# Attention into expert FFNs: q scaled on DVE, reciprocals spread by TensorE, one casting load queue, program order

## The chip, the cores and the metric

One core of one Trainium2 chip. The time is the device time in microseconds (us) of one execution. Engines: PE is TensorE (matmul), PEld its weight loads, DVE is VectorE, ACT is ScalarE, POOL is GpSimd, SP is SyncE. "Block j" means the FFN of expert 0 on 512 tokens; a block's start is the first matmul into `h_ps` of that block, FFN1 are its matmuls into `h_ps` and FFN2 those into `y_ps`. The releaser of a wait is what ended it. The granted clock is the share of the full TensorE clock that the profile shows. An attend computes a piece of `xT` for one batch. A slot is a place between two groups of FFN matmuls where other work may be put.

## The reference, cut to what matters

```python
# q, k, v: (8 batches, 8 heads, 576, 64);  E = 8 experts, Dm = 512, F = 1024, N = 4608 tokens
q_p = concat(relu(q) * cos, relu(q) * sin)       # 128 features; k_p alike; cos, sin depend on the position
kv  = einsum('bhsf,bhsd->bhfd', k_p, v);  z = k_p.sum(over positions)
num = einsum('bhsf,bhfd->bhsd', q_p, kv); den = einsum('bhsf,bhf->bhs', q_p, z) + 1e-6
x   = num / den                                   # then (B*S, H*D) = (4608, 512)
P   = exp(x @ w_gate);  P = sinkhorn(P, 8 rounds) # over all 4608 tokens
out = sum over e of P[:, e] * (relu(x @ w1[e]) @ w2[e])
```

The routing needs the gates of all tokens, so the FFNs of experts 1 to 7 can't be weighted before attention is finished. The kernel therefore runs expert 0, unweighted, while attention is still being prepared.

## The kernel before

Batch b+1 and b+2 are prepared while the FFN of block b runs. The parts that matter are these.

```python
# turn: q is transposed and multiplied by cos / sin in one go, by half-width matmuls
for c in range(i * C3, (i + 1) * C3):
    for a in range(2):
        nc.tensor.matmul(out=t_ps[a * D : (a + 1) * D, ...], lhsT=q16[:, c, :], rhs=cs_diag[:, c, a, :], ...)
# ... then relu from PSUM into q_pT, on ACT and DVE by turns

# denominators: 96 rows x 192 reciprocals, copied to 128 partitions by a trip through DRAM
nc.vector.reciprocal(out=den[:], in_=den[:])
for j in range(3):
    nc.scalar.dma_start(out=r_dram[:, j, :], in_=den[32 * j : 32 * j + H, :])
rb = acc_hi[...]                       # borrowed from the tail of the output accumulator
for hh in range(2):
    nc.scalar.dma_start(out=rb[hh * HP : (hh + 1) * HP], in_=r_dram[hh : H : 2]. ... .to_broadcast([HP, HK, S]))

# attend: xT = num * rb
nc.vector.tensor_tensor(out=xT[...], in0=num_ps[...], in1=rbs[b][...], op=ALU.mult)

# loads: q cast to fp16 by the GpSimd queue, k and v as fp32 on the SP queue, 4 buffers each;
# the weights of expert 0 stand in the GpSimd queue between the q loads of batch 0 and batch 1
```

The order of the instructions on each engine is left to a scheduler, which does not keep the order of the program text.

The softmax here doesn't subtract the row's maximum and nothing guards it: scores larger than these inputs give would overflow.

Of the kernel before, what the change touches and what calls it, by code (L numbers as in the profile page):

```python
# [9 lines left out]
FP32 = mybir.dt.float32  # L10
# [12 lines left out]
def kernel(  # L23
# [39 lines left out]
    ps_h = ctx.enter_context(tc.tile_pool(name="ps_h", bufs=3, space=bass.MemoryType.PSUM))  # L63
    ps_y = ctx.enter_context(tc.tile_pool(name="ps_y", bufs=2, space=bass.MemoryType.PSUM))
    ps_s = ctx.enter_context(tc.tile_pool(name="ps_s", bufs=3, space=bass.MemoryType.PSUM))

    xT = xT_pool.tile([P, KT, N], F16, name="xT")

    G_LO = NG - 8
    acc_lo = acc_pool.tile([P, G_LO, Dm], FP32, name="acc_lo")  # L70
    acc_hi = acc_pool.tile([P, NG - G_LO, Dm], FP32, name="acc_hi")

    def acc(g):
        return acc_lo[:, g, :] if g < G_LO else acc_hi[:, g - G_LO, :]
# [3 lines left out]
    def load_weights(pool, e, cuts):  # L78
        w1e = pool.tile([P, KT, F], F16, name="w1e")
        w2e = pool.tile([P, FT, Dm], F16, name="w2e")  # L80
        v1 = moe_w1[e].rearrange("(kt p) f -> p kt f", p=P)
        v2 = moe_w2[e].rearrange("(ft p) d -> p ft d", p=P)
        for i in range(cuts):
            f0, f1 = i * F // cuts, (i + 1) * F // cuts
            nc.gpsimd.dma_start(out=w1e[:, :, f0:f1], in_=v1[:, :, f0:f1])  # L85
        for i in range(cuts):
            f0, f1 = i * FT // cuts, (i + 1) * FT // cuts
            nc.gpsimd.dma_start(out=w2e[:, f0:f1, :], in_=v2[:, f0:f1, :])  # L88
        return w1e, w2e


    def ffn1(hT, w, j, fts=range(FT)):
        for ft in fts:
            h_ps = ps_h.tile([P, TCH], FP32, name="h_ps")
            for kt in range(KT):
                nc.tensor.matmul(  # L96
                    out=h_ps[:],
                    lhsT=w[0][:, kt, ft * P : (ft + 1) * P],
                    rhs=xT[:, kt, j * TCH : (j + 1) * TCH],
                    start=(kt == 0),  # L100
                    stop=(kt == KT - 1),
                )
            nc.scalar.activation(out=hT[:, ft, :], in_=h_ps[:], func=AF.Relu)  # L103

    def ffn2(hT, e, w, j, tss=range(TCH // P)):
        for ts in tss:
            g = j * TCH // P + ts
            y_ps = ps_y.tile([P, Dm], FP32, name="y_ps")
            for ft in range(FT):
                nc.tensor.matmul(  # L110
                    out=y_ps[:],
                    lhsT=hT[:, ft, ts * P : (ts + 1) * P],
                    rhs=w[1][:, ft, :],
                    start=(ft == 0),
                    stop=(ft == FT - 1),
                )
            if e == 0:

                if g % 2 == 0:
                    nc.scalar.copy(out=acc(g), in_=y_ps[:])  # L120
                else:
                    nc.vector.tensor_copy(out=acc(g), in_=y_ps[:])
            else:
                nc.vector.scalar_tensor_tensor(  # L124
# [12 lines left out]
    with ExitStack() as p1:  # L137
        cs_pool = p1.enter_context(tc.tile_pool(name="cs_pool", bufs=1))
        ld = p1.enter_context(tc.tile_pool(name="ld", bufs=4))
        kp_pool = p1.enter_context(tc.tile_pool(name="kp_pool", bufs=3))  # L140
        va_pool = p1.enter_context(tc.tile_pool(name="va_pool", bufs=3))
        qT_pool = p1.enter_context(tc.tile_pool(name="qT_pool", bufs=8))
        kv_pool = p1.enter_context(tc.tile_pool(name="kv_pool", bufs=2))

# [3 lines left out]
        def load(b, hk):  # L148
            t = []
            for name, src, dt, eng in (  # L150
                ("q", q, F16, nc.gpsimd), ("k", k, FP32, nc.sync), ("v", v, FP32, nc.sync),
            ):
                x = ld.tile([P, C, D], dt, name=f"{name}_ld")
                view = src[b].rearrange("(hk hh) (p c) d -> (hh p) hk (c d)", hh=2, c=C)
                eng.dma_start(out=x[:].rearrange("p c d -> p (c d)"), in_=view[:, hk])  # L155
                t.append(x)
            loaded[b, hk] = t

        for hk in range(HK):
            load(0, hk)  # L160


        half_pi = cs_pool.tile([P, 1], FP32, name="half_pi")
        nc.vector.memset(half_pi[:], float(np.pi / 2.0))
# [5 lines left out]
        )  # L170
        wrap = cs_pool.tile([P, C], FP32, name="wrap")
        nc.vector.tensor_scalar(
# [3 lines left out]
        nc.vector.scalar_tensor_tensor(  # L176
# [6 lines left out]
        nc.scalar.activation(out=cs[:, :, 0, :], in_=s_b, func=AF.Sin, bias=half_pi[:], scale=-ang)  # L183
        nc.scalar.activation(out=cs[:, :, 1, :], in_=s_b, func=AF.Sin, scale=ang)
        ident = cs_pool.tile([P, P], F16, name="ident")
        nc.gpsimd.memset(ident[:], 1.0)
        nc.gpsimd.affine_select(
            out=ident[:], in_=ident[:], pattern=[[-1, P]], compare_op=ALU.is_equal,
            fill=0.0, base=0, channel_multiplier=1,
        )  # L190

        cs_diag = cs_pool.tile([P, C, 2, P], F16, name="cs_diag")
        nc.vector.tensor_tensor(  # L193
            out=cs_diag[:].rearrange("p c a s -> p (c a) s"),
            in0=ident[:].unsqueeze(1).to_broadcast([P, 2 * C, P]),
            in1=cs[:, :, :, 0:1].rearrange("p c a o -> p (c a) o").to_broadcast([P, 2 * C, P]),
            op=ALU.mult,
        )
# [3 lines left out]
        nc.vector.memset(zmask[:], 0.0)  # L202
        for h in range(H):
            nc.vector.memset(zmask[:, h, h : 32 : H], 1.0)
        ones_col = const.tile([P, 1], FP32, name="ones_col")
        nc.vector.memset(ones_col[:], 1.0)
        scale_row = const.tile([1, 2, P], FP32, name="scale_row")
        nc.vector.memset(scale_row[:, 0, :], float(N) / float(E))
        nc.vector.memset(scale_row[:, 1, :], float(N) / float(E) / XS)
# [3 lines left out]
        nc.vector.tensor_copy(out=wg[:], in_=wg_ld[:])  # L213

        w0 = load_weights(wA, 0, 4)


        kps, qTs, kvs, rbs = {}, {}, {}, {}

        def prep(b, hk):  # L220
            _, k32, v32 = loaded[b, hk]
            v_aug = va_pool.tile([P, C, D + 2], F16, name="v_aug")
            nc.vector.tensor_copy(out=v_aug[:, :, 0:D], in_=v32[:])  # L223
            nc.vector.memset(v_aug[:, :, D : D + 1], 1.0 / XS)
            k16 = kp_pool.tile([P, C, D], F16, name="k16")
            nc.scalar.activation(out=k16[:], in_=k32[:], func=AF.Relu)
            k_p = kp_pool.tile([P, C, 2, D], F16, name="k_p")
            nc.vector.tensor_tensor(  # L228
                out=k_p[:], in0=k16[:].unsqueeze(2).to_broadcast([P, C, 2, D]),
                in1=cs[:], op=ALU.mult,  # L230
            )
            kps[b, hk] = (k_p, v_aug)

        C3 = C // 3

        def turn(b, hk, i):

            q16 = loaded[b, hk][0]
# [3 lines left out]
            for c in range(i * C3, (i + 1) * C3):  # L242
                for a in range(2):
                    nc.tensor.matmul(  # L244
                        out=t_ps[a * D : (a + 1) * D, (c - i * C3) * P : (c - i * C3 + 1) * P],
                        lhsT=q16[:, c, :],
                        rhs=cs_diag[:, c, a, :],
                        start=True,
                        stop=True,
                    )  # L250
            dst = qTs[b, hk][:, i * C3 : (i + 1) * C3, :].rearrange("p c s -> p (c s)")
            if (3 * hk + i) % 2 == 0:
                nc.scalar.activation(out=dst, in_=t_ps[:, 0 : C3 * P], func=AF.Relu)  # L253
            else:
                nc.vector.tensor_scalar(  # L255
# [3 lines left out]
        def sums(b, half):  # L259
# [8 lines left out]
            for i in range(2):  # L268
                k_p, v_aug = kps.pop((b, 2 * half + i))
                for c in range(C):  # L270
                    for hh in range(2):
                        nc.tensor.matmul(  # L272
# [6 lines left out]
            for hh in range(2):  # L279
                kv_v = kv_ps[hh][:, 0 : 2 * (D + 1)].rearrange("p (hk d) -> p hk d", d=D + 1)  # L280
                nc.vector.tensor_tensor(  # L281
# [5 lines left out]
                nc.scalar.copy(out=kv_sb[:, 2 * half : 2 * half + 2, hh, :], in_=kv_v[:, :, 0:D])  # L287

        def denominators(b):
# [3 lines left out]
            for h in range(H):  # L293
                hk, hh = h // 2, h % 2
                for j in range(3):
                    nc.tensor.matmul(  # L296
# [7 lines left out]
            nc.vector.tensor_scalar(  # L304
# [3 lines left out]
            nc.vector.reciprocal(out=den[:], in_=den[:])  # L308
            r_dram = dram.tile([H, 3, C3 * HP], FP32, name="r_dram")
            for j in range(3):  # L310
                nc.scalar.dma_start(out=r_dram[:, j, :], in_=den[32 * j : 32 * j + H, :])
            rb = acc_hi[:].rearrange("p g d -> p (g d)")[:, 0 : HK * S].rearrange(
                "p (hk s) -> p hk s", hk=HK
            )
            for hh in range(2):
                nc.scalar.dma_start(  # L316
                    out=rb[hh * HP : (hh + 1) * HP],
                    in_=r_dram[hh : H : 2].rearrange("(o hk) j s -> o hk (j s)", o=1)
                    .to_broadcast([HP, HK, S]),
                )  # L320
            rbs[b] = rb
# [3 lines left out]
        def by_place(ap):  # L325
            return ap.rearrange("p (c ph s) -> p ph c s", ph=2, s=HQ)

        def attend(b, hk, ph):
            num_ps = ps_s.tile([P, 512], FP32, name="small_ps")
            for hh in range(2):  # L330
                p0 = hh * HP + ph * HQ
                nc.tensor.matmul(  # L332
# [6 lines left out]
            nc.vector.tensor_tensor(  # L339
                out=by_place(xT[:, hk, b * S : (b + 1) * S])[:, ph],  # L340
                in0=num_ps[:, 0 : C * HQ].rearrange("p (c s) -> p c s", s=HQ),
                in1=by_place(rbs[b][:, hk, :])[:, ph],
# [3 lines left out]
        def gates(b):  # L346
            g0, g1 = b * S // P, (b + 1) * S // P
            lg_ps = ps_s.tile([P, 512], FP32, name="small_ps")
            for g in range(g0, g1):
                for kt in range(KT):  # L350
                    nc.tensor.matmul(
# [6 lines left out]
            nc.scalar.activation(  # L358
# [7 lines left out]
        NS = FT + TCH // P  # L366
# [5 lines left out]
        def collect(b, first):  # L372

            res = []
            for hk in range(HK):
                if hk % 2 == 0:
                    res.append((prep, (b, hk)))
                    res.append((prep, (b, hk + 1)))
# [118 lines left out]
```

## Time and profile before

1143.69 us (median of 3, 1143.29 to 1143.71). The profiled execution has a span of 1141.9 us.

| stretch (before), us | what runs | TensorE busy |
|---|---|---|
| 0 to 59 | attention of batches 0 and 1 alone | 21.86 of 59 |
| 84.6 to 204.53 | blocks 1 to 5, attention in between | 115.70 of 119.93 |
| 204.53 to 230.00 | block 6 | 20.12 of 25.47 |
| 230.00 to 244.59 | block 7, nothing left to prepare | 14.59 of 14.59 |
| 248 to 1141 | the remaining FFNs | 886.43 of 893 |

Lines of the page of the kernel before: the busy times, then each engine's busy share in 40 equal slices of the span (in tenths, 9 is 90% or more), with the granted TensorE clock and the DMA share.

```profile
PE 1086.9 (95%) x6256; PEld 500.5 (44%) x6256; DVE 337.7 (30%) x591; ACT 403.8 (35%) x719; POOL 90.7 (8%) x97
...
PE   2499999899999999999999999999999999999998
...
PEclk9999999999999999999999999999999999999999
DMA  9956663604000400013000400031000400013333
```

TensorE is the bottleneck. Of its 55 us of idle time (1141.9 minus 1086.9), 37 lie in the first 59 us and 5.4 in block 6, the gap in the eighth slice. So read the start and the gap, not the average. The list of waits says what TensorE stood for (engine, line, releaser: total us, times, longest).

```profile
PE small_ps L244 <- DVE cs_diag L193: 18.2, 1, 18.2
PE small_ps L332 <- DVE xT L339: 14.2, 2, 9.4
PE small_ps L244 <- DMA q_ld<-in_q_dram: 6.6, 1, 6.6
PE small_ps L244 <- DVE xT L339: 2.9, 4, 1.1
```

DVE's timeline at the start (start, us, engine, line, operation; in brackets the idle time before it and its releaser) shows how one wait feeds the next.

```profile
29.81 0.35 DVE L304 TENSOR_SCALAR den<-small_ps 96x192 f32<-96x192 f32 x1
36.77 0.56 DVE L255 TENSOR_SCALAR q_pT<-small_ps 128x384 f16<-128x384 f32 x1 [6.61 <-PE small_ps L244]
37.24 1.34 DVE L308 RECIPROCAL den<-den 96x192 f32<-96x192 f32 x1
...
55.59 1.92 DVE L339 TENSOR_TENSOR xT<-small_ps,acc_hi 128x288 f16<-128x288 f32 x5 [7.04 <-DMA acc_hi<-r_dram]
```

The denominators of batch 0 were ready at 30.2 us. Their reciprocal ran at 37.24, because it stood in DVE's order behind an eviction of batch 1, which waited for a matmul, which waited for a q load stuck behind the weights. Then came the trip through DRAM: the store was issued at 38.6, the load at 42.8, and the first `xT` ran at 55.59.

The gap is block 6, where the trip is exposed once more (timeline of TensorE, kernel before).

```profile
217.95 1.89 PE L110 MATMUL y_ps<-w2e,hT 128*128 128x512 f16 x8 [0.24 <-ACT acc_lo L120]
224.56 1.18 PE L332 MATMUL small_ps<-q_pT,kv_sb 128*64 128x288 f16 x6 [4.72 <-DVE xT L339]
225.88 3.57 PE L110 MATMUL y_ps<-w2e,hT 128*128 128x512 f16 x8
```

TensorE stands 4.72 us, and the next eight FFN matmuls take 3.57 us where the eight before took 1.89.

### The profile page before, as it was taken

The numbers are of one execution on the slowest core, as the hardware profiler recorded it, in microseconds if no ns is written. First come the engines' busy times: TensorE is split into PE (matmuls) and PEld (weight loads), VectorE is DVE, ScalarE is ACT, GpSimd is POOL, SyncE is SP. The second block draws the span as 40 slices with busy tenths as digits, with TensorE's granted clock in tenths as the row PEclk, the third lists the DMA queues.
The fourth block names the chain that finished last, engine by engine and source line by source line (L and its number), as shares of the span: only waits on it lengthen the run. The fifth ranks groups of instructions, "written<-read, shape, count | busy, mean of one in ns | idle before, by whom it ended". The sixth has DMA issues, their size and how long they took to land.

```text
span 1141.9 us, 14695 instructions
## 1 busy us (share of the span) xinstructions
PE 1086.9 (95%) x6256; PEld 500.5 (44%) x6256; DVE 337.7 (30%) x591; ACT 403.8 (35%) x719; POOL 90.7 (8%) x97
## 2 busy tenths in 40 slices
PE   2499999899999999999999999999999999999998
PEld 2344444344444444444444444444444444444443
DVE  5466665245222222222222222222222222222222
ACT  4244443232333333333333333333333333333332
POOL 3000100004950000000000000000000000000000
PEclk9999999999999999999999999999999999999999
DMA  9956663604000400013000400031000400013333
GB/s 262 250 142 160 154 157 78 117 4 71 1 1 1 74 1 1 1 20 55 1 1 1 74 1 1 1 56 19 1 1 8 67 1 1 1 27 78 81 74 74
DMA packets 39090, 60.36 MB, mean 53 GB/s; under 512 B 4016, under 2 KB 18544, under 8 KB 39024
## 3 DMA queue, kind: packets, MB, share of 16 engines
q0 software_dynamic: 18784, 21.50, 12.5%
q1 hardware_dynamic: 15504, 28.34, 9.1%
q10 hardware_dynamic: 4736, 9.59, 3.7%
q8 instruction: 49, 0.80, 0.3%
q14 instruction: 17, 0.14, 0.0%
HBM read 71.32 MB, written 9.58 MB: 71 GB/s over the span
## 4 chain that ended last, share of the span: by engine, by line
PE 87%; DMA 8%; DVE 3%; issue 1%; ACT 0%; POOL 0%; ACTq 0%; DVEq 0%; POOLq 0%
PE h_ps L96 42%; PE y_ps L110 41%; DMA acc_hi<-r_dram 5%; DMA q_ld<-in_q_dram 1%; PE small_ps L244 1%; DMA w1e<-in_moe_w_dram 1%; PE small_ps L332 1%; PE small_ps L272 1%; PE small_ps L296 1%; DMA r_dram<-den 0%; DVE colp L431 0%; DVE xT L339 0%; DVE P_tok L426 0%; ACTq L316 0%; DVE k_p L228 0%
## 5 line engine op out<-in xcount | busy, mean ns | idle before, releaser
L103 ACT ACTIVATE hT<-h_ps 128x512 f16<-128x512 f32 x576 | 342.9, 598 | 635.0 <-PE h_ps L96 625.7
L110 PE MATMUL y_ps<-w2e,hT 128*128 128x512 f16 x2304 | 520.8, 380 | 1.9 <-DVE acc_lo L124 0.7
L96 PE MATMUL h_ps<-xT,w1e 128*128 128x512 f16 x2304 | 520.1, 380 | 0.0
L110 PEld LDWEIGHTS <-hT 128*128 128x128 f16 x2304 | 222.5, 98 | 269.1 <-issue 4.8
L96 PEld LDWEIGHTS <-w1e 128*128 128x128 f16 x2304 | 221.3, 98 | 266.1 <-issue 5.7
L124 DVE SCALAR_TENSOR_TENSOR acc_lo<-y_ps,P_tok,acc_lo 128x512 f32<-128x512 f32 x196 | 147.2, 751 | 522.8 <-PE y_ps L110 518.7
L124 DVE SCALAR_TENSOR_TENSOR acc_hi<-y_ps,P_tok,acc_hi 128x512 f32<-128x512 f32 x56 | 42.1, 751 | 151.3 <-PE y_ps L110 151.3
L244 PE MATMUL small_ps<-cs_diag,q_ld 128*64 128x128 f16 x576 | 32.0, 246 | 29.6 <-DVE cs_diag L193 18.2
L85 POOL DMA_DIRECT2D w1e<-in_moe_w_dram x11 | 8.4, 765 | 594.8 <-PE h_ps L96 568.3
L459 POOL TENSOR_SCALAR acc_lo<-acc_lo,P_tok 128x512 f32<-128x512 f32 x28 | 43.1, 1553 | 10.4 <-DVE P_tok L441 10.4
L244 PEld LDWEIGHTS <-q_ld 128*64 128x64 f16 x576 | 22.1, 122 | 49.4 <-issue 35.6
L255 DVE TENSOR_SCALAR q_pT<-small_ps 128x384 f16<-128x384 f32 x48 | 26.4, 554 | 46.2 <-PE small_ps L244 46.2
L339 DVE TENSOR_TENSOR xT<-small_ps,acc_hi 128x288 f16<-128x288 f32 x64 | 25.7, 450 | 27.3 <-DMA acc_hi<-r_dram 25.2
L253 ACT ACTIVATE q_pT<-small_ps 128x384 f16<-128x384 f32 x48 | 23.8, 495 | 24.7 <-PE small_ps L244 23.6
L332 PE MATMUL small_ps<-q_pT,kv_sb 128*64 128x288 f16 x128 | 17.3, 328 | 15.8 <-DVE xT L339 14.2
L155 POOL DMA_DIRECT2D q_ld<-in_q_dram x32 | 17.1, 537 | 150.7 <-PE small_ps L244 149.4
L223 DVE CAST v_aug<-v_ld 128x576 f16<-128x576 f32 x32 | 23.9, 748 | 11.0 <-DMA v_ld<-in_v_dram 8.7
L332 PEld LDWEIGHTS <-kv_sb 128*64 128x64 f16 x128 | 6.8, 112 | 30.8 <-issue 30.4
L272 PE MATMUL small_ps<-v_aug,k_p 64*128 64x65 f16 x576 | 16.8, 203 | 0.6 <-ACT q_pT L253 0.5
L272 PEld LDWEIGHTS <-k_p 64*128 64x128 f16 x576 | 14.9, 102 | 3.6 <-issue 2.8
L287 ACT CAST kv_sb<-small_ps 128x128 f16<-128x128 f32 x32 | 7.0, 264 | 17.2 <-DVE zsel L281 17.2
L88 POOL DMA_DIRECT2D w2e<-in_moe_w_dram x11 | 9.1, 823 | 42.5 <-PE y_ps L110 32.6
(131 smaller groups left out, 168.4 us busy)
## 6 DMA issues: line engine op xcount, KB each, us to landing
k_ld<-in_k_dram SPq DMA_DIRECT2D x32, 288.0 KB
v_ld<-in_v_dram SPq DMA_DIRECT2D x32, 288.0 KB
acc_hi<-r_dram ACTq DMA_DIRECT2D x16, 576.0 KB
w1e<-in_moe_w_dram POOLq DMA_DIRECT2D x7, 1024.0 KB, 8.4
w2e<-in_moe_w_dram POOLq DMA_DIRECT2D x7, 1024.0 KB, 9.2
out_dram<-acc_lo SPq DMA_DIRECT2D x56, 128.0 KB
q_ld<-in_q_dram POOLq DMA_DIRECT2D x32, 144.0 KB, 4.0
out_dram<-acc_hi SPq DMA_DIRECT2D x16, 128.0 KB
```

Of the source, the lines that this page charges most:

```text
L96: nc.tensor.matmul(out=h_ps[:], lhsT=w[0][:, kt, ft * P : (ft + 1) * P], rhs=xT[:, kt, j * TCH : (j + 1) * TCH], start=(kt == 0), stop=(kt ...
L103: nc.scalar.activation(out=hT[:, ft, :], in_=h_ps[:], func=AF.Relu)
L110: nc.tensor.matmul(out=y_ps[:], lhsT=hT[:, ft, ts * P : (ts + 1) * P], rhs=w[1][:, ft, :], start=(ft == 0), stop=(ft == FT - 1),)
L124: nc.vector.scalar_tensor_tensor(out=acc(g), in0=y_ps[:], scalar=P_tok[:, g, e : e + 1], in1=acc(g), op0=ALU.mult, op1=ALU.add,)
L223: nc.vector.tensor_copy(out=v_aug[:, :, 0:D], in_=v32[:])
L244: nc.tensor.matmul(out=t_ps[a * D : (a + 1) * D, (c - i * C3) * P : (c - i * C3 + 1) * P], lhsT=q16[:, c, :], rhs=cs_diag[:, c, a, :], sta ...
L253: nc.scalar.activation(out=dst, in_=t_ps[:, 0 : C3 * P], func=AF.Relu)
L255: nc.vector.tensor_scalar(out=dst, in0=t_ps[:, 0 : C3 * P], scalar1=0.0, scalar2=None, op0=ALU.max)
L272: nc.tensor.matmul(out=kv_ps[hh][:, i * (D + 1) : (i + 1) * (D + 1)], lhsT=k_p[hh * HP : (hh + 1) * HP, c].rearrange("p a d -> p (a d)"), ...
L332: nc.tensor.matmul(out=num_ps[hh * HP : (hh + 1) * HP, 0 : C * HQ], lhsT=kvs[b][0][:, hk, hh, :], rhs=qTs[b, hk][:, :, p0 : p0 + HQ], star ...
L339: nc.vector.tensor_tensor(out=by_place(xT[:, hk, b * S : (b + 1) * S])[:, ph], in0=num_ps[:, 0 : C * HQ].rearrange("p (c s) -> p c s", s=H ...
L459: nc.gpsimd.tensor_scalar(out=acc(g), in0=acc(g), scalar1=P_tok[:, g, 0:1], scalar2=None, op0=ALU.mult,)
```

## The change

It makes five alterations at once, beside some in the sizes of buffers.

1. q is multiplied by cos and sin on DVE (`q_p`), and turned by full-width matmuls against the identity. This replaces the table `cs_diag`.
2. The reciprocals are no longer sent through DRAM. Each is split into a high and a low fp16 part, lying in different rows, and a matmul with a matrix of zeros and ones adds the two and copies them to 64 partitions.
3. All loads of q, k and v go through the one casting queue, in order of need, with 7 buffers; the gate weights stay on the SP queue.
4. The attention and expert-0 blocks are written in program order, which is then kept on TensorE, DVE and ACT. Before, the scheduler chose.
5. The plan of what is prepared in which slot is new: batch 1 is prepared in one lump between FFN1 and FFN2 of block 0, and the later batches in finer slots (16 to a block instead of 12, since FFN2 is cut in halves).

In this part `small_ps` has 4 buffers instead of 3 and `h_ps` 2 instead of 3, and some SBUF pools changed their depth.

```diff
+    class InOrder:                      # every call is kept in program order
+        def __getattr__(self, name):
+            def call(*args, **kwargs):
+                return tc.keep_in_program_order(getattr(self.engine, name)(*args, **kwargs))
+            return call
+    te, ve, se = bound                  # TensorE, DVE, ACT; set free again after the attention part
...
-                ("q", q, F16, nc.gpsimd), ("k", k, FP32, nc.sync), ("v", v, FP32, nc.sync),
+            for name, src in (("q", q), ("k", k), ("v", v)):   # all F16, all nc.gpsimd
...
+        w0 = new_weights(wA)
+        load_w1(w0, 0, 4)
+        for hk in range(HK):
+            load(1, hk)
+        load_w2(w0, 0, 4)
...
-        cs_diag = cs_pool.tile([P, C, 2, P], F16, name="cs_diag")
+            ve.tensor_tensor(out=q_p[:], in0=loaded[b, hk][0][:]. ... , in1=cs[:], op=ALU.mult)
...
-                for a in range(2):
-                    nc.tensor.matmul(out=t_ps[a * D : (a + 1) * D, ...], lhsT=q16[:, c, :], rhs=cs_diag[:, c, a, :])
+                te.matmul(out=t_ps[:, ...], lhsT=qps[b, hk][:, c], rhs=ident[:])
...
-            for j in range(3):
-                nc.scalar.dma_start(out=r_dram[:, j, :], in_=den[32 * j : 32 * j + H, :])
-            (two loads of r_dram, broadcast to 64 partitions each)
+            ve.tensor_copy(out=hi[:], in_=den[:])
+            ve.scalar_tensor_tensor(out=hl[:], in0=hi[:], scalar=lo[0:96], in1=den[:], op0=ALU.mult, op1=ALU.add)
...
+            for j in range(3):          # in attend, 8 times per batch
+                te.matmul(out=rb_ps[:, ...], lhsT=spread[0:96, j, hk], rhs=hls[b][...])
+            se.copy(out=rb[:], in_=rb_ps[:, 0 : C * HQ])
...
+        at(0, FT - 1, whole, 1)         # batch 1 as one lump after FFN1 of block 0
+        at(0, FT, gates, 0)
```

## The prediction

> **What bounds it now.** The page shows TensorE busy 1086.9 of 1141.9 us, so only its idle or wasted time can be won. The table of windows splits the span. From about 248 us on, 32 FFN matmuls take 6.91 us (216 ns each), without slack; the change leaves these alone. In 0-59 us TensorE works only 23 us: the list of waits has it waiting 18.2 us for the diagonal table cs_diag (queued on DVE behind the 16 KB gate load), 6.6 us for a q load stuck behind weights in the casting queue, and 9.4 us for xT, which waits for the reciprocals' trip through DRAM. Then come six blocks of about 24.4 us (FFN part 64 x 0.216 = 13.8 us) with only some 1.4 us idle each, mostly xT waiting for that trip. In block 6 the trip is exposed: TensorE stands 4.7 us at 219.8 us, then runs eight matmuls at 0.43 us instead of 0.216 (granted clock 0.83-0.87). Block 7 ends at 244.5 us.
>
> **Costs per block.** The turn's 64-column matmuls already run in pairs: 12 start within 0.36-0.46 us, 30-38 ns each, so 72 cost 2.2-2.7 us. 36 full-width ones at an estimated 58 ns cost 2.1 us: almost nothing won. (The Trainium skill, "TensorE: Matmul & The Clock Gate", Part 3, says column tiles run concurrently; this trace agrees.) Spreading adds 24 matmuls of 96 columns, estimated 1.3 us, and eight ACT copies (estimated 0.40 us each). DVE gets four q multiplies of 0.75 us and hi/lo casts (0.6 us), and its v casts shrink from 0.75 to an estimated 0.3: about 18.6 us per block; ACT 16. Program order is now kept. So a block costs 23.4 us of TensorE plus some 0.5 us of in-order stalls: 23.9, only 0.5 us better.
>
> **Start.** The casting queue moves about 160 GB/s of results at full share (windows at 254 and 263 us). One batch of q, k, v is 1.77 MB, 11 us; so batch 0 is in at about 15 us, w1 22, batch 1 33, w2 39. DVE needs 11 us per batch. First FFN matmul at about 29 us (was 56.9), FFN1 until 38, partly at half clock. Then batch 1 is prepared as one lump: ACT has a relu for batch 2's k ahead of it, landing at about 41 us, and TensorE mostly waits until about 54. FFN2 of block 0 ends at about 66. Six blocks: 209. Block 7 without the stall: 224 instead of 244.5. The Sinkhorn stage and later keep their order of matmuls (compared). All of the gain is counted at the end of block 7, on the critical path in full.
>
> **Prediction: 1121 us, range 1106 to 1135. Chances: faster by over 2% 0.48, within 2% 0.50, slower 0.02.**
>
> **What would show it.** Right: first h_ps matmul at 26-33 us; no DMA among what xT waits for; between the first FFN1 and FFN2 over 8 us of sparse small matmuls; blocks 1-6 at 23-24.6 us; no stall before block 7; 6.91 us per 32 matmuls after 250 us; turn's TensorE time about as before. Wrong: blocks below 22.5 us (turn or switching cheaper) or above 25 (DVE, or its order holding small_ps buffers); block 0 ending before 58 or after 74 us.
>
> **What would make it wrong.** The 160 GB/s might not hold for 2304-byte rows; the lump of batch 1 may hide better or worse; half clock through the sparse start could add 3-5 us; engines in order could lock step, above all ACT copy and DVE multiply with two rb buffers. The gain is near the 2% line (22.9 us), hence the split.

## The result, and the profile after

The new kernel takes 1114.28 us (median of 4, 1113.66 to 1114.99), the old one beside it on the same chip 1143.70. The ratio is 0.9737 (95% interval 0.9719 to 0.9756): faster by 2.6%. Ratios here are the mean time of one kernel's fast runs over that of the other's of the same rounds, so they are not quite the ratio of the medians. The profiled span is 1112.0 us.

Lines of the page of the kernel after, to be held against those before:

```profile
PE 1084.9 (98%) x6160; PEld 509.4 (46%) x6160; DVE 355.3 (32%) x642; ACT 427.7 (38%) x782; POOL 124.8 (11%) x160
...
PE   5899999999999999999999999999999999999998
...
PEclk9899999999999999999999999999999999999999
DMA  9955510440002200040002200040002200013333
```

TensorE's busy time fell by only 2 us, but its idle time fell from 55 to 27 us (1112.0 minus 1084.9). What it still waits for (list of waits, kernel after; most instructions of this part carry line 82, that of the helper, so go by the tiles):

```profile
PE small_ps L82 <- DVE q_p L82: 10.3, 3, 5.8
PE small_ps L82 <- ACT q_pT L82: 3.6, 5, 2.3
PE small_ps L82 <- DVE hl L82: 2.6, 1, 2.6
```

`cs_diag`, the q load and `xT` are gone from it. And DVE's `xT` waits for no DMA any more (list of DVE's waits, kernel after):

```profile
DVE xT L82 <- ACT rb L82: 19.8, 35, 1.2
```

The start as TensorE saw it (timeline, kernel after):

```profile
28.37 8.34 PE L82 MATMUL h_ps<-xT,w1e 128*128 128x512 f16 x32
36.54 0.67 PE L82 MATMUL small_ps<-ident,q_p 128*128 128x128 f16 x9
39.99 0.68 PE L82 MATMUL small_ps<-ident,q_p 128*128 128x128 f16 x9 [2.79 <-DVE q_p L82]
...
49.42 1.89 PE L82 MATMUL y_ps<-w2e,hT 128*128 128x512 f16 x4
...
61.85 1.03 PE L82 MATMUL h_ps<-xT,w1e 128*128 128x512 f16 x4
```

FFN1 starts at 28.37 us (it was 56.85). The lump of batch 1 lasts from 36.54 to 49.42. TensorE is busy in 8.07 of these 12.88 us, at a granted clock of 0.68 (table of windows), so part of that busy time is slow work. Block 1 starts at 61.85.

Here is where the blocks start, and from that where the gain lies:

| | block 0 | block 1 | block 7 | end of block 7 |
|---|---|---|---|---|
| before, us | 56.85 | 84.60 | 230.00 | 244.59 |
| after, us | 28.37 | 61.85 | 200.81 | 215.35 |
| after minus before | -28.5 | -22.8 | -29.2 | -29.2 |

So 22.8 us come from the start. The other 6.4 come from blocks 1 to 6, which took 145.4 us and now take 139.0; block 6 with the exposed trip gives 2.6 of that (25.5 against 22.8), the other five 3.8. From block 7 on nothing changes: the whole gain of 29.2 us arrives at the end, where the span is 29.9 us shorter. Note that 5.7 of the 28.5 us at block 0's start were given back by its end: batch 1, which the old kernel prepared before block 0, is now a lump inside it.

### The profile page after: what moved, and what is told of

Read it like the earlier page. It is cut to its first block, busy times and chain, and to the rows that moved or that the text cites. A ratio compares the mean times of both kernels' runs of the same rounds, so it can differ in the third digit from the quotient of the medians.

```text
span 1112.0 us, 14620 instructions
## 1 busy us (share of the span) xinstructions
PE 1084.9 (98%) x6160; PEld 509.4 (46%) x6160; DVE 355.3 (32%) x642; ACT 427.7 (38%) x782; POOL 124.8 (11%) x160
## 3 DMA queue, kind: packets, MB, share of 16 engines
q0 software_dynamic: 28000, 30.94, 18.2%
## 4 chain that ended last, share of the span: by engine, by line
PE 90%; DVE 4%; DMA 3%; issue 1%; POOL 1%; ACT 0%; POOLq 0%; ACTq 0%; DVEq 0%
PE y_ps L131 39%; PE h_ps L116 39%; PE y_ps L82 5%; PE small_ps L82 4%; PE h_ps L82 3%; DMA q_ld<-in_q_dram 1%; DMA v_ld<-in_v_dram 1%; DMA w2e<-in_moe_w_dram 1%; DVE k_p L82 1%; DVE q_p L82 0%; DVE colp L504 0%; DVE q_pT L82 0%; DMA k_ld<-in_k_dram 0%; DVE v_aug L82 0%; DVE P_tok L499 0%
## 5 line engine op out<-in xcount | busy, mean ns | idle before, releaser
L146 DVE SCALAR_TENSOR_TENSOR out_acc<-y_ps,P_tok,out_acc 128x512 f32<-128x512 f32 x252 | 189.3, 751 | 674.1 <-PE y_ps L131 670.0
L533 POOL TENSOR_SCALAR out_acc<-out_acc,P_tok 128x512 f32<-128x512 f32 x36 | 55.4, 1553 | 10.1 <-DVE P_tok L514 10.1
L82 ACT ACTIVATE hT<-h_ps 128x512 f16<-128x512 f32 x64 | 38.3, 599 | 22.8 <-PE h_ps L82 22.4
L82 PE MATMUL small_ps<-ident,q_p 128*128 128x128 f16 x288 | 28.3, 234 | 14.4 <-DVE q_p L82 10.3
L82 ACT COPY rb<-small_ps 128x288 f32<-128x288 f32 x64 | 25.6, 400 | 27.3 <-PE small_ps L82 21.0
L82 DVE TENSOR_TENSOR xT<-small_ps,rb 128x288 f16<-128x288 f32 x64 | 29.1, 455 | 20.7 <-ACT rb L82 19.8
L82 PEld LDWEIGHTS <-hT 128*128 128x128 f16 x256 | 21.1, 98 | 25.5 <-issue 0.9
L82 PEld LDWEIGHTS <-q_p 128*128 128x128 f16 x288 | 20.8, 104 | 24.9 <-DVE q_p L82 11.4
L82 DVE TENSOR_TENSOR k_p<-k_ld,cs 128x1152 f16<-128x1152 f16 x32 | 24.0, 751 | 10.8 <-ACT k_ld L82 10.8
L82 ACT ACTIVATE k_ld<-k_ld 128x576 f16<-128x576 f16 x32 | 21.8, 685 | 6.2 <-DMA k_ld<-in_k_dram 6.2
L82 DVE TENSOR_TENSOR q_p<-q_ld,cs 128x1152 f16<-128x1152 f16 x32 | 24.0, 749 | 0.3 <-DMA q_ld<-in_q_dram 0.2
```

The source lines that it names most:

```text
L82: return tc.keep_in_program_order(getattr(self.engine, name)(*args, **kwargs))
L146: ve.scalar_tensor_tensor(out=acc(g), in0=y_ps[:], scalar=P_tok[:, g, e : e + 1], in1=acc(g), op0=ALU.mult, op1=ALU.add,)
L533: nc.gpsimd.tensor_scalar(out=acc(g), in0=acc(g), scalar1=P_tok[:, g, 0:1], scalar2=None, op0=ALU.mult,)
```

## The experiments

Twelve kernels were run, all gave correct results. Those named b_ are the old kernel with a part of the change, those named a_ the new kernel with a part undone or altered. Four jobs were run (b_gate to b_both; a_diag to a_mix; a_act to a_pe; a_mixact); the old kernel's medians in them were 1143.91, 1145.14, 1144.55 and 1146.56 us, and each ratio is to those of its own job.

The claims to be told apart: (A) my theory, that the gain is loads in order of need plus the reciprocals kept off DRAM, while the form of the turn and program order are near neutral; (B) that the `cs_diag` wait of 18.2 us was the gate load, so moving that load alone would pay; (C) that the turn by full-width matmuls is what pays; (D) that program order is what pays.

### b_gate: old kernel, gate weights loaded first

```diff
+        (load of wg_ld and the cast into wg moved here)
         for hk in range(HK):
             load(0, hk)
```

> The kernel before, with only the 16 KB load of the gate weights and its cast moved ahead of the q, k, v loads, so that cs_diag no longer stands behind it on DVE. Waits-add theory: the largest wait in the list (18.2 us of TensorE for cs_diag) shrinks by about 10 us and the time with it, to about 1133 us. My theory: the first turn comes at about 8-10 us, but the next waits (a q load behind the weights until about 36 us, then the reciprocals' trip through DRAM) take it all back; first h_ps matmul still at 54-57 us, time 1140-1144 us.

Measured: 1145.87 us, ratio 1.0023 (0.9988 to 1.0057): no gain, and claim B falls. But the expected path was wrong too. The first turn did not come at 8 to 10 us, since the wait for `cs_diag` hardly shrank (17.3 instead of 18.2 us); so this run can't show whether later waits would have taken the gain back. DVE's timeline in this run shows why:

```profile
2.78 0.28 DVE L162 CAST wg<-wg_ld 128x32 f16<-128x32 f32 x1 [1.25 <-DMA wg_ld<-in_moe_w_gate_dram]
6.26 0.75 DVE L224 CAST v_aug<-v_ld 128x576 f16<-128x576 f32 x1 [3.20 <-DMA v_ld<-in_v_dram]
...
12.18 0.75 DVE L224 CAST v_aug<-v_ld 128x576 f16<-128x576 f32 x1 [1.65 <-DMA v_ld<-in_v_dram]
12.85 0.16 DVE L177 TENSOR_SCALAR wrap<-gidx 128x9 f32<-128x9 f32 x1
...
14.71 2.56 DVE L198 TENSOR_TENSOR cs_diag<-ident,cs 128x2304 f16<-128x2304 f16 x1 [1.49 <-ACT cs L189]
```

The gate cast is out of the way at 2.78 us, yet the tiny `wrap`, the first step towards `cs_diag`, runs at 12.85, behind three casts of v that wait for their loads. A small table stood at the tail of the line because of where the scheduler had put it. The prediction's words "queued on DVE behind the 16 KB gate load" named only the last thing in that line, worth under 1 us.

### b_loads, b_spread, b_both: old kernel with the loads, with the spread, with both

```diff
 b_loads:   k and v cast by the GpSimd queue like q; order w1, batch 1, w2; ld bufs 4 -> 7
 b_spread:  hi / hl on DVE, three spread matmuls and an ACT copy into rb in attend; no r_dram
            (rb lies in the region of acc_hi that the old kernel borrowed, for want of other SBUF space)
 b_both:    both edits; turn, schedule and plan of slots as in the old kernel
```

> The kernel before, with only the loads changed: k and v cast to fp16 in the same queue as q, in the order batch 0, w1, batch 1, w2, with seven buffers. My theory: no q load behind weights, and the reciprocal on DVE no longer stands behind an eviction that waits for it; fewer bytes in the way of the trip through DRAM, which falls from 12 us to about 6. First h_ps matmul at 40-46 us, stalls in the blocks stay, time 1126-1133 us. Rival (the trip through DRAM is the whole cost of the start): at most 4 us gained.

> The kernel before, with only the reciprocals changed: spread by TensorE from hi/lo rows, with an ACT copy, instead of the trip through DRAM. My theory: first h_ps matmul at about 46-49 us (the reciprocal still comes at about 37 us on DVE), no stall of 4.7 us before block 7, but blocks of about 24 us since the idle time removed is paid in TensorE work: 1126-1132 us. Rival (spread is the source of nearly all of the gain): 1114-1118 us.

> The kernel before, with both the loads and the spread of the reciprocals changed, but the turn with half-width matmuls, no program order, two batches prepared before the first FFN matmul. If turn, program order and schedule give nothing: 1114 plus or minus 3 us. My theory: the new schedule gives some: batch 1 is prepared before FFN begins here as in the kernel after, first h_ps at 36-40 us, block 0 ends at about 62 us, blocks of about 24 us, time 1116-1122 us.

| run | us | ratio (95%) | block 1 starts | blocks 1 to 6 |
|---|---|---|---|---|
| b_loads | 1134.96 | 0.9924 (0.9895 to 0.9953) | 78.34 | 143.9 |
| b_spread | 1137.33 | 0.9943 (0.9914 to 0.9972) | 79.05 | 144.7 |
| b_both | 1130.65 | 0.9892 (0.9867 to 0.9917) | 71.65 | 145.1 |
| new kernel | 1114.28 | 0.9737 (0.9719 to 0.9756) | 61.85 | 139.0 |

All three gained less than expected. Claim A falls: the two parts together give 13 us of the 29, and some 16 us are left for the rest of the change (9.8 before block 1, 6.1 in blocks 1 to 6). The spread does remove the stall of block 6 (19.2 us instead of 25.5), but it makes the ordinary blocks longer: blocks 1 to 3 take 25.3 us on average in b_spread, 25.5 in b_both and 24.5 in the old kernel. The next runs ask what the missing 16 us are.

### a_diag: new kernel, turn done the old way

```diff
+        cs_diag = ...                                  # as before, early in DVE's program order
-            ve.tensor_tensor(out=q_p[:], ...)          # no multiplication of q
-                te.matmul(out=t_ps[:, ...], lhsT=q_p, rhs=ident)
+                for a in range(2):
+                    te.matmul(out=t_ps[a * D : (a + 1) * D, ...], lhsT=q16[:, c, :], rhs=cs_diag[:, c, a, :])
```

> The kernel after, with only the turn undone: q as loaded, half-width matmuls against the diagonal table cs_diag, no q multiply on DVE. My theory: half-width pairs run side by side, 72 of them take about as long as 36 full-width ones (2.0-2.5 us per block), DVE is not the limit: 1112-1118 us; cs_diag (2.55 us on DVE) costs up to 2 us at the start. Rival (full-width turns halve the turn's TensorE time): 2 us and more per batch, 1128 us or more.

Measured: 1114.80 us, ratio 0.9741 (0.9725 to 0.9758), the same as the new kernel. Claim C falls. The intervals of the two ratios overlap widely, so the turn is worth no more than about 3 us. In block 2: 23.64 us with half-width turns, 23.17 with full-width ones. Blocks 1 to 6 get cheaper by 2.7 us in all, and the start 0.5 us dearer; there TensorE waits 10.3 us for `q_p`, in a_diag 6.1 for `cs_diag`.

### a_dram: new kernel, reciprocals through DRAM again

```diff
-            (hi, hl, spread matmuls, ACT copy)
+            for j in range(3):
+                nc.sync.dma_start(out=r_dram[:, j, :], in_=den[32 * j : 32 * j + H, :])
+            for hh in range(2):
+                nc.sync.dma_start(out=rb[hh * HP : (hh + 1) * HP], in_=r_dram[...] broadcast)   # one buffer, in acc_hi
```

It uses the SP queue, not ACT's as the old kernel did, and keeps program order.

> The kernel after, with only the spread of the reciprocals undone: they go through DRAM again, issued by the otherwise empty SP queue, into a single buffer. My theory: the trip lies open, since the first attend comes two slots after the denominators: 4-6 us at the start and about 3-4 us in each of seven blocks, less about 2 us of TensorE work per block for spread matmuls no longer done: 1122-1135 us. Rival (the trip hides under FFN work and the spread's own matmuls cost as much as they save): 1108-1116 us.

Measured: 1185.31 us, ratio 1.0356 (1.0334 to 1.0378): a miss by 50 us. Lines of DVE's timeline in one block of this run:

```profile
93.32 1.35 DVE L84 RECIPROCAL den<-den 96x192 f32<-96x192 f32 x1
94.59 0.69 DVE L84 TENSOR_TENSOR q_p<-q_ld,cs 128x1152 f16<-128x1152 f16 x1
106.78 1.19 DVE L84 TENSOR_TENSOR xT<-small_ps,acc_hi 128x288 f16<-128x288 f32 x3 [11.50 <-DMA acc_hi<-r_dram]
```

TensorE's timeline just after:

```profile
107.29 0.45 PE L84 MATMUL small_ps<-q_pT,kv_sb 128*64 128x288 f16 x2 [7.45 <-DVE xT L84]
107.67 1.89 PE L84 MATMUL y_ps<-w2e,hT 128*128 128x512 f16 x4
```

The trip takes 12.1 us (store issued at 94.69, `xT` at 106.78), and `xT` stands in DVE's fixed order ahead of other work: DVE idles 11.5 us, though ACT had finished a relu of k, which the `k_p` behind `xT` reads, by 95.2. TensorE waits for `xT` 72.6 us in all, eight times, and runs the next FFN matmuls at 0.45 us instead of 0.22. So the two parts depend on each other. Under the scheduler's order and the old plan, the spread saves about 4 us (b_loads 1134.96 to b_both 1130.65, with intervals that overlap); under program order and the new plan it saves 71 us (1185.31 to 1114.28). In this plan, program order can be kept because the slow trip is gone. The new plan also gives the trip less time: its first attend comes three slots of 16 after the denominators, in the old plan nine of 12. How much of the 71 us is the fixed order and how much this short notice was not separated. Nor can this run give the trip's cost in the old kernel, where the scheduler hid most of it.

### a_free: new kernel, program order lifted

```diff
-                return tc.keep_in_program_order(getattr(self.engine, name)(*args, **kwargs))
+                return getattr(self.engine, name)(*args, **kwargs)
```

> The kernel after, with only the program order lifted: the scheduler may place TensorE, DVE and ACT work of the first part as it likes. If program order is a main source of the gain: 1124 us or more, with more idle time in blocks 1-6. My theory: 1112-1120 us, since the emission order is the same and the waits are short.

Measured: 1133.17 us, ratio 0.9898 (0.9871 to 0.9926). My theory (1112 to 1120) missed, the alternative held: with all else in place, program order is worth 19 us. In the profiled executions, 7.6 us lie before block 1 and 12.5 in blocks 1 to 6. The new plan without program order is thus no faster than b_both (1130.65); program order with the old plan was not run. Claim D is right as far as it goes. But an order is a property of one engine; the next three runs ask which.

### a_act, a_pedve, a_pe: program order kept on some engines only

```diff
-    te, ve, se = bound
+    te, ve, se = nc.tensor, nc.vector, InOrder(nc.scalar)            # a_act
+    te, ve, se = InOrder(nc.tensor), InOrder(nc.vector), nc.scalar   # a_pedve
+    te, ve, se = InOrder(nc.tensor), nc.vector, nc.scalar            # a_pe
```

Two ideas: that a relu of k, placed on ACT before the load it needs has landed, blocks everything behind it on ACT; or that the order of TensorE or DVE matters. In a_pedve TensorE and DVE keep the new kernel's order; only ACT's differs.

> The new kernel with program order kept on ACT alone; TensorE and DVE free again. Lifting it on all three cost 19 us (1133.2 against 1114.3). If the loss is the head of ACT's line (a relu of k placed ahead of the data it waits for, with q_pT, rb and hT behind it), keeping ACT's order gets nearly all of it back: 1114 to 1120 us, blocks 1 to 6 near 23.5 us. If it is the order of TensorE (finer mixing of FFN and small matmuls, more switches) or of DVE (q_p, k_p and the hi/lo rows behind xT), the time stays at 1126 to 1135 us.

> The new kernel with program order kept on TensorE and DVE, ACT free. Head of ACT's line as the cause: 1126 to 1135 us, with ACT standing on a load of k while q_pT or rb wait. Order of TensorE or DVE as the cause: 1114 to 1120 us.

> The new kernel with program order kept on TensorE alone, DVE and ACT free. Head of ACT's line as the cause: 1126 to 1135 us. Order of TensorE as the cause: 1114 to 1120 us, blocks near 23.3 us. Order of DVE as the cause: above 1126 us here, with the run that keeps TensorE and DVE at 1114 to 1120.

| run | order kept on | us | ratio (95%) | block 1 starts | blocks 1 to 6 |
|---|---|---|---|---|---|
| new kernel | TensorE, DVE, ACT | 1114.28 | 0.9737 (0.9719 to 0.9756) | 61.85 | 139.0 |
| a_act | ACT | 1110.23 | 0.9696 (0.9668 to 0.9723) | 60.30 | 137.0 |
| a_pedve | TensorE, DVE | 1132.02 | 0.9889 (0.9857 to 0.9921) | 68.28 | 149.3 |
| a_pe | TensorE | 1134.71 | 0.9924 (0.9884 to 0.9964) | 71.62 | 148.8 |
| a_free | none | 1133.17 | 0.9898 (0.9871 to 0.9926) | 69.45 | 151.4 |

The split is clean: in these five, with ACT's order kept the kernel is fast, without it slow (a_act even came out 4 us below its range). ACT's waits for loads of k tell why. From the list of ACT's waits in a_free:

```profile
ACT k_ld L82 <- DMA k_ld<-in_k_dram: 46.7, 29, 4.6
```

The same list in a_pedve:

```profile
ACT k_ld L260 <- DMA k_ld<-in_k_dram: 41.5, 28, 5.9
```

And in a_act:

```profile
ACT k_ld L82 <- DMA k_ld<-in_k_dram: 5.4, 3, 2.7
```

Free, ACT stands for a load of k on nearly every one of the 32 relus; in order, on three (in the new kernel too: 6.2 us, 3 times). How that reaches TensorE shows in a_pedve. ACT's timeline in one block:

```profile
98.50 0.68 ACT L260 ACTIVATE k_ld<-k_ld 128x576 f16<-128x576 f16 x1 [1.91 <-DMA k_ld<-in_k_dram]
99.09 0.47 ACT L303 ACTIVATE q_pT<-small_ps 128x384 f16<-128x384 f32 x1
```

TensorE's timeline at the same time:

```profile
99.61 0.50 PE L82 MATMUL small_ps<-ident,q_p 128*128 128x128 f16 x6 [1.38 <-ACT q_pT L303]
```

ACT idles 1.91 us for a load that has not landed; the eviction of `q_pT` behind it (the relu that takes it from PSUM to SBUF) runs at 99.09; TensorE, which needs the buffer of `small_ps` that this frees, stands 1.38 us. Kept in program order, the relus of the next batch's k run in the last ten slots of a block, when their loads are in.

No run moved the relus of k alone, and ACT's free order differs in one other place too (twice a block, an eviction of `q_pT` moves ahead of two copies into `kv_sb`). But the traces hold a control. Free, the relus run a block or more earlier, so blocks 5 and 6 have none left, while the other difference remains there. Lines of the table of windows for block 4 (four relus of k in it) and block 5 (none) of a_pedve, then block 5 of the new kernel (four too, with their loads in; columns as explained below):

```profile
144.68:171.30 26.62, 23.06 (x256) 12.53 (x253) 17.55 (x41) 14.18 (x33) 4.78 (x9) 1.00 0.41 59
171.30:194.92 23.62, 22.91 (x260) 12.60 (x257) 18.12 (x43) 12.32 (x29) 0.00 (x0) 1.00 0.01 1
154.71:177.98 23.27, 22.92 (x260) 12.55 (x257) 17.61 (x41) 14.55 (x33) 0.00 (x0) 1.00 0.00 1
```

Blocks 5 and 6 together take 46.0 to 46.3 us in a_free, a_pe, a_pedve and 46.1 in the new kernel. All of the 10 to 12.5 us that these runs lose in blocks 1 to 6 is lost in blocks 1 to 4, where the relus run. For the 6 to 10 us lost before block 1 there is no such control.

The same sign is in the old kernel's descendants: with k in the casting queue, ACT waits for it 19.3 us (10 times) in b_loads and 18.2 (13 times) in b_both, and in b_both TensorE waits 14.3 us for `q_pT` on ACT, where the new kernel waits 3.6. That fits, but the order of ACT alone was not altered in b_both, so for those 16 us it is argued, not shown.

Keeping TensorE and DVE in program order too seems slightly harmful on the whole: a_act is 4 us below the new kernel (from different jobs, with intervals that just overlap at 0.972; the spans are 1108.5 and 1112.0 us). A block with TensorE and DVE free takes 22.5 us with no idle time at all. Lines of the table of windows for one block each (window, length, busy time of PE, PEld, DVE, ACT, POOL with their counts, clock, DMA share, GB/s), in the new kernel:

```profile
85.11:108.28 23.17, 22.82 (x255) 12.46 (x253) 17.61 (x41) 14.54 (x33) 6.33 (x13) 1.00 0.55 79
```

In a_act:

```profile
84.98:107.48 22.50, 22.50 (x257) 12.41 (x253) 17.92 (x41) 14.64 (x33) 6.37 (x12) 1.00 0.60 80
```

In a_pedve:

```profile
93.34:119.35 26.01, 23.05 (x255) 12.54 (x253) 17.38 (x41) 14.18 (x33) 6.36 (x12) 1.00 0.50 70
```

The new kernel has 0.35 us of idle TensorE in its block, a_act none, and a_pedve 2.96, with nearly the same work. Those 2.96 us are three waits for `q_pT` on ACT (0.45, 1.38 and 1.13), each behind a relu of k that had stood for its load.

Whether TensorE's or DVE's freedom gives those 4 us was not separated.

### a_mix: new kernel, batch 1 prepared in pieces

```diff
-        at(0, FT - 1, whole, 1)
+        early = {2: prep_k, 4: prep_q, 6: prep_kv}       # between the last attends of batch 0
+        for slot, items in enumerate((                    # turns, sums and the rest, in the FFN1 slots of block 0
+            ((prep_k, 1), (turn, 0, 0), (turn, 0, 1), (prep_q, 1)), ...
```

> The kernel after, with batch 1 no longer prepared as one lump between FFN1 and FFN2 of block 0 but spread over the last attends of batch 0 and the slots of FFN1 of block 0. My theory: in the kernel after the lump lasts 13 us (36.5 to 49.4 us) with about 5.5 us of TensorE work in it, and batch 1 is in SBUF long before; so FFN2 of block 0 starts at 41-44 us instead of 49.4 and the time falls by 5-8 us to 1106-1109 us. Rival (DVE and ACT are the limit there, or the data comes too late): within 2 us of 1114.

Measured: 1105.87 us, ratio 0.9662 (0.9647 to 0.9678), just under the expected range. FFN1 still starts at 28.33, but FFN2 starts at 40.88 instead of 49.42, and block 1 at 53.86 instead of 61.85. The other blocks are as in the new kernel. So the lump cost 8 us, and TensorE had FFN work to fill it with. Block 0 in the table of windows, first of the new kernel, then of a_mix:

```profile
28.37:61.85 33.48, 28.66 (x261) 16.00 (x260) 21.50 (x50) 18.41 (x39) 14.00 (x27) 0.85 0.91 142
28.33:53.86 25.53, 24.49 (x260) 13.17 (x259) 20.72 (x49) 17.29 (x38) 14.34 (x27) 1.00 1.14 189
```

Only half of the 8 us is idle time (4.8 us before, 1.0 now). The other half is clock: TensorE's busy time falls from 28.66 to 24.49 us for the same work, at a granted clock of 1.00 instead of 0.85. This beats both kernels.

### a_mixact: both improvements together

```diff
+        (the edit of a_mix)
-    te, ve, se = bound
+    te, ve, se = nc.tensor, nc.vector, InOrder(nc.scalar)
```

> The version that came of the two best runs: batch 1 prepared between the last attends of batch 0 and the FFN1 slots of block 0, and program order kept on ACT alone. Against the new kernel's 1114.3 us the first was worth 8.4 us and the second 4.1 us. If they add, 1101 to 1103 us: blocks 1 to 6 at 22.5 us and block 0 at 25 us. If a free TensorE already fills the lump of batch 1 by itself, so that the two gains are partly the same one, 1104 to 1109 us.

Measured: 1107.63 us, ratio 0.9662 (0.9646 to 0.9679): they don't add, and the result equals a_mix's. Blocks 1 to 6 do take 134.9 us instead of a_mix's 138.9, as hoped. But FFN1 begins at 32.78 us instead of 28.33, and block 1 at 60.08 instead of 53.86. DVE's timeline at the start of a_mixact shows what puts the FFN off:

```profile
20.94 0.76 DVE L265 TENSOR_TENSOR q_p<-q_ld,cs 128x1152 f16<-128x1152 f16 x1 [2.86 <-DMA q_ld<-in_q_dram]
21.61 0.34 DVE L331 TENSOR_TENSOR zsel<-zmask,small_ps 128x64 f16<-128x64 f16 x2
25.89 1.34 DVE L358 RECIPROCAL den<-den 96x192 f32<-96x192 f32 x1
```

And of a_mix:

```profile
20.30 1.35 DVE L82 RECIPROCAL den<-den 96x192 f32<-96x192 f32 x1
```

It is the same fault on another engine: DVE, now free, has a `q_p` of batch 1 ahead of batch 0's `zsel`, and that `q_p` stands for its load. The reciprocals come 5.6 us later, and TensorE stands 6.12 us for `hl` behind them. (In a_act the reciprocal runs at 25.02, so there too.) The second expectation also fits: block 0 takes 27.1 us in a_act and 27.3 here, so with TensorE and DVE free, a_mix's edit gains nothing in block 0. The reading that follows, and that no run tested, is that order should be kept on all three engines up to block 1 and on ACT alone after it; 53.86 plus 134.9 would then put block 7 at about 189 us, an estimate from these two runs, 4 us ahead of a_mix's 192.81.

## Why the prediction was right or wrong

The time fell in the range and on the right side of the line: 1121 predicted, 1114.28 measured, 6.7 us too pessimistic. Faster had been given a chance of 0.48. The total was near; some of the reasons were not. Summed up, the terms of the text gave 1123 (224 instead of 244.5 at the end of block 7), and 1121 was put down; the terms were thus 8.7 us too pessimistic there (224 against 215.35), some 4 us by the end of block 0 and 4 in blocks 1 to 6.

- **What bounds the kernel: right.** All of the gain is in the first 245 us and reaches the end in full (29.2 us at the end of block 7, 29.9 in the span).
- **First FFN matmul at 29 us: right** (28.37).
- **Lump: right in kind, too long by 3 us.** FFN1 was to end at 38 and FFN2 to start at 54; measured 36.5 and 49.4. The relu for batch 2's k was expected to hold ACT until that load landed at 41 us; it ran at 36.37, right behind a relu of the FFN. So block 0 ended at 61.85, not 66. The half clock that the prediction feared is there: 0.68 in the lump, worth some 4 us by the comparison with a_mix.
- **Blocks at 23.9 us: slightly too high** (23.2 to 23.3 for blocks 1 to 5). Six blocks make some 4 us. The mis-sized term is TensorE's work, 22.8 to 22.9 us instead of 23.4; the in-order stalls were 0.35 us, not 0.5. The prediction said "only 0.5 us better"; on average over six blocks they are 1.1 us better (24.2 became 23.2).
- **Turn near neutral: right.** Twelve half-width matmuls took 0.46 us from start to start (38 ns each), six full-width ones 0.34 (56 ns each); the new form takes half as many. a_diag confirms: same time within about 3 us.
- **Spread at 1.3 us a block: right or too low, by how it is measured.** In b_spread TensorE is busy 24.66 us in block 1 where the old kernel has 23.37: 1.3 us more. Taken from start to start, two attends took 0.36 us in the old kernel (204.17 to 204.53) and take 0.94 in the new one (52.43 to 53.37), which would make 2.3 us for the eight of a block. In b_spread and b_both it shows as blocks 0.8 to 0.9 us longer, although the waits for the trip were gone.
- **DVE and ACT: off the limit in a block, as predicted.** They work 17.6 and 14.5 us a block (predicted 18.6 and 16). The ACT copy takes 0.40 us as estimated, the v cast 0.45 instead of 0.3.
- **"Program order is now kept ... some 0.5 us of in-order stalls": the step that failed.** Program order was booked as a small cost. For TensorE and DVE together it is one on the whole (a_act is 4 us better without). For ACT it is worth 18 to 23 us (a_pedve against the new kernel, a_free against a_act). The prediction knew the mechanism in one place (the relu of batch 2's k at the head of ACT's line) but had no term for what the scheduler would have done to the new plan of loads. The number did not suffer, because the new kernel fixes the order; the account of where the gain comes from did. Without that order the same plan takes 1133 us.
- **"queued on DVE behind the 16 KB gate load": wrong as a cause.** b_gate moved that load and gained nothing; what stood ahead of `cs_diag` were three casts waiting for v.
- **No stall before block 7: right**, and no DMA is among the releasers of `xT`.

Where the 29 us come from can't be written as a sum of parts. Loads give 9 us alone, spread 6.6 us alone, both 13 us; program order on all three engines earns 19 us without the trip, while with the trip the new plan in program order is 40 us slower than the old kernel.

## What to carry to other kernels

Read the order of each engine, not only its busy time: one instruction that waits for a load that has not landed holds all those behind it, and ACT, busy 38% of the span in a_free, cost about 20 us that way without looking busy. When a change removes a slow path (a DRAM trip), try again the schedules that were too slow with it; and when it fixes the order on all engines, free them again one at a time, because the gain may be one engine's and the others may pay for it; look at each stage by itself, since here a free DVE cost over 4 us at the start, while a free TensorE and DVE gained time later. Preparing in one lump what can be put between matmuls in pieces leaves the bottleneck idle: here 8 us for moving a few calls.

## What the Trainium skill lacked or had wrong

- "TensorE: Matmul & The Clock Gate", "Back-to-back issue gap", gives a sustained roofline of about 131 ns per matmul of N=512 and about 81 ns for N=128, and says the formula of the isolated gap (216 and 56 ns) over- and under-counts. This case agrees with the formula and not with the roofline: 32 FFN matmuls of 512 columns take 6.91 us, 216 ns each, with their weight loads, over hundreds of us; six full-width turns of 128 columns start within 0.34 us, 56 ns each.
- The same page, Part 3, says that column tiles run concurrently, which the trace agrees with, and gives measured gains for three tiles and more, none for two halves of 64. Here a pair of half-width turns takes 76 ns (12 in 0.46 us), one full-width turn that does the same 56 ns, and undoing the full-width form moved the kernel by no more than about 3 us.
- The same page, Part 1, ties the drop to half clock to an idle window of about 3.4 us. Stands of 4.72 us (kernel before) and 7.45 us (a_dram) agree: the next FFN matmuls take 0.45 us instead of 0.22. In a_free four FFN matmuls took 1.89 us at 114.10 us although the longest wait shortly before was 1.56 us; that fits the page's section on a second failure mode, short idles between groups, but the page gives no figure for how many are enough.
- "VectorE: DVE Perf Modes", the perf-mode tier table, has `tensor_copy` at 4x for 16-bit data and 2x for fp32, 693 and 1227 ns for 2048 elements. Here the copy of v went from 0.748 us (fp32 source, cast to fp16) to 0.447 us (fp16 source) for 576 elements per partition, into rows of 64 in steps of 66. The ratio, 1.7, is close to the table's 1.77. The table has no entry for a copy that also casts, or for rows with gaps.
- "DMA: Bandwidth & Descriptors" gives a fixed cost of about 2 us for one DMA. It has no figure for a small store (three DMAs of 6 KB) and a broadcast load that depends on it (two of 576 KB), which here took 12.1 us from the first issue to the first use in a_dram, and 17.0 us at the start of the kernel before (38.6 to 55.59), where other loads ran too (DMA share 0.99 from 28 to 59 us).
- No page that was read says that an engine's place in line is the thing to check when a schedule is left to software; the number here is 46.7 us of ACT waiting for loads in a_free against 6.2 us in the new kernel.
